# An earlier first search, one-hots in one comparison per quarter, and a new place for the first expert in the plan

## The chip, the cores and the metric

The kernel runs on one core of a Trainium2 chip. The metric is the device time of one execution in microseconds: 1155.01 us is the median of three runs (1153.06, 1155.01 and 1155.10). TensorE (PE) multiplies, VectorE (DVE), ScalarE (ACT) and GpSimd (POOL) do elementwise work, and SyncE (SP) issues most of the transfers. Each engine takes its instructions in the order in which they were written to its queue.

## The reference

Three layers follow one another. Attention with a sink and a window gives `x` for N = 3072 tokens of 512 features. A dense layer `x = g(x @ w_in) @ w_out` follows. The last one shares the tokens out to 8 experts of 384 tokens each, which this change is about:

```python
    cap = N // E
    logits = x @ w_gate
    order = np.argsort(-flat)                  # flat = logits.flatten()
    for idx in order:
        tok, e = (int(idx) // E, int(idx) % E)
        if assigned[tok] >= 0 or counts[e] >= cap:
            continue
        assigned[tok] = e
        counts[e] += 1
    ...
        h = np.maximum(x[mask] @ w1[e], 0.0)
        out[mask] = h @ w2[e]
```

## The kernel before

The tokens go through the dense layer in 12 blocks of 256 (`moe1_steps`). A block makes 16 hidden pieces `f` (`hid`: 12 products into `hp`, then VectorE, ScalarE and GpSimd make `u` and its parts `gh` and `gl`) and adds each piece's share of the outcome (`proj`: 12 products into `up`, in a low and a high half of the columns; the high half also holds the logits). Every fp32 product is done as three products of rounded parts. The last block first makes only its logits (`gate`, `logits`), and its outcome (`rows`) is made while the first search runs. The rows go to a table in memory, `x2d` (`done`).

The tokens of one expert are found by a search (`phase`). `values` (`v`) and `owners` (`own`) take each token's best logit and its expert. Seven rounds narrow a threshold down: `compare` (`ind`, 768 comparisons in a partition), `count` (`pg`, six products), `counts` (`cnt`), `total` (`pc`), `bound` (`hit` to `th`). Then `above`, `loads`, `choose` and `rank` choose the expert whose share is full and number its tokens, `places`, `slots` (`oh`, a one-hot matrix of 128 places for each of 24 tiles) and `look` (`pk`, 24 products) turn the numbers into a list, `tokens` (`tok`) writes it as integers, and `retire` takes these tokens and the expert out of the logits for the next search. `gather` has GpSimd fetch the 384 rows (`xg`), `turn` turns them round on TensorE (`xt`) and splits them (`xsh`, `xsl`). `weight` loads an expert's weights (`w1r`, `w2r`) and splits them into a high and a low part: the low part (`w1l`, `w2l`) either by VectorE (`rest`) or by a transfer that adds to a negated copy (`minus`, `add`). `expert` multiplies (`hp`, then `us`) and `store` writes the rows out.

Eight experts run after one another, and the search of the next stands between the products of the one before. `experts` sets that order with a table of times: `at(t, step)` puts a step at time t of a plan, the plan is sorted, and in what `at` enters every engine keeps the sorted order. The times only set an order; how long something takes is not in them. `T[k]` is the place of expert k's first product, `PERIODS` the length of an expert, `SECOND` the place of the second search after the first one's end, `CHAIN` the distance from one search to the next. The products of the last two blocks and the first search are entered without that rule: there the building layer sorts by its own priorities. `unread` writes products that nobody reads (`idle`) where TensorE has no work.

Of the kernel before, what the change touches and what calls it, by code (L numbers as in the profile page):

```python
# [7 lines left out]
F32 = mybir.dt.float32  # L8
# [48 lines left out]
FIND = 21.5  # L57
PERIODS = [39.5] * (E - 2) + [37.0, 33.5]

SECOND, CHAIN, EARLY = 11.3, 34.8, 59.0  # L60
# [7 lines left out]
NQ = 4  # L68

# [5 lines left out]
class Kernel:  # L75
# [547 lines left out]
    def moe1_steps(self, blk, xs, hold=None, part=None):  # L623
# [5 lines left out]
        fa, fz = part or (0, FT)  # L629
        hps, ahead = {}, blk > 1  # L630
# [17 lines left out]
        def hid(f):  # L648
# [22 lines left out]
        def proj(f):  # L671
            gh, gl = st.pop(f)
            assert f in self.have_out
            if f == fa:
# [68 lines left out]

        store = [(0.0, lambda: done(0)), (0.0, lambda: done(1))]
        second = gate if hold else proj
# [10 lines left out]
        rest = []  # L756
# [10 lines left out]
    def pools2(self, e):  # L767
        tc = self.tc
        self.oh = e(tc.tile_pool(name="oh", bufs=1))
        self.ex = e(tc.tile_pool(name="ex", bufs=2))  # L770
        self.ew = e(tc.tile_pool(name="ew", bufs=2))

    def router_consts(self):
# [8 lines left out]
        self.nrow = rt.tile([P, P], BF16, name="nrow")  # L782
# [15 lines left out]
        self.t_row = rt.tile([P, GT], F32, name="t_row")  # L798
        nc.vector.tensor_copy(self.t_row, fl[:, 0, :GT])
# [20 lines left out]
    def phase(self, last, out, first=False):  # L820
# [5 lines left out]
        def values():  # L826
            v = st["v"] = self.rw.tile([P, GT], F32, name="v")
            nc.vector.tensor_reduce(out=v, in_=lm, axis=AX.X, op=OP.max)
# [4 lines left out]
        def owners():  # L833
            st["own"] = self.rw.tile([P, GT, E], BF16, name="own")
            nc.vector.tensor_tensor(out=st["own"], in0=lm, in1=st["v"].unsqueeze(2).to_broadcast([P, GT, E]),
                                    op=OP.is_equal)
# [4 lines left out]
        def compare(r):  # L841
            n = 1 << ROUNDS[r][1]
            th = st["th"] if r else self.pat[0]
            ge = st["ind"] = self.rw.tile([P, GT, n], BF16, name="ind", tag=f"ind{n}")
            nc.vector.tensor_tensor(out=ge, in0=st["v"].unsqueeze(2).to_broadcast([P, GT, n]),  # L845
                                    in1=th.bitcast(F32).unsqueeze(1).to_broadcast([P, GT, n]), op=OP.is_ge)
# [8 lines left out]
        def count(r):  # L855

            n = 1 << ROUNDS[r][1]
            pg = st["pg"] = self.psum([g * n, g * E], self.rtag, "pg")
            for t in range(0, GT, g):
# [108 lines left out]
        def places():  # L968
# [6 lines left out]
            nc.vector.scalar_tensor_tensor(a, a, -float(P), z, op0=OP.mult, op1=OP.add)  # L975
# [5 lines left out]
            st["oh"] = self.oh.tile([P, GT, P], BF16, name="oh", bufs=1)  # L981
            st["a"] = a
            st["pk"] = self.psum([P, 6], "A", "pk")
# [3 lines left out]
        def slots(h):  # L987
            for t in range(n_ * h, n_ * h + n_):
                nc.vector.tensor_scalar(st["oh"][:, t], self.nrow, st["a"][:, t:t + 1], None, op0=OP.is_equal)  # L989

        def look(h):
            for t in range(n_ * h, n_ * h + n_):
                nc.tensor.matmul(st["pk"], st["oh"][:, t], st["rr"][:, t].rearrange("p x c -> p (x c)"),
                                 start=(t == 0), stop=(t == GT - 1))
                if first and t < GT - 1:
                    self.unread(1, 5 * 32)
            if h == NQ - 1:
                st["tf"] = self.rw.tile([P, 3], F32, name="tf")
                nc.scalar.copy(st["tf"], st["pk"][:, 0:3])
# [8 lines left out]
    def weight(self, cur, i, first):  # L1008
# [4 lines left out]
        dma = name == "w2" or (first and c == 0)  # L1013
# [64 lines left out]
    def expert(self, cur):  # L1078
# [6 lines left out]
        def up(f):  # L1085
# [5 lines left out]
            def part(i):  # L1091
                w_, x_ = ((wl, xh), (wh, xl), (wh, xh))[i]
# [59 lines left out]
    def experts(self, plan, start):  # L1152
# [17 lines left out]
        def find(k, ph, t):  # L1170
# [8 lines left out]
            for r in range(len(ROUNDS)):  # L1179
# [4 lines left out]
                at(t + 1.0, ph["count"], r)  # L1184
                free.append(t + 1.05)
                at(t + 1.35 + GAP, ph["counts"], r)
                free.append(t + 1.45 + GAP)
                at(t + 1.6 + GAP, ph["total"], r)
                at(t + 2.05 + 2 * GAP, ph["bound"], r)
# [4 lines left out]
        for k in range(E):  # L1194
            cur, ph = curs[k], self.phase(k + 1 == E, curs[k], k == 0)
            if k == 0:

                steps = [(1.0, ph["values"]), (1.0, ph["owners"])]
                for r in range(len(ROUNDS)):
                    steps += [(1.0, lambda r=r, f=ph[n]: f(r)) for n in ("compare", "count", "counts", "total", "bound")]  # L1200
# [353 lines left out]
```

## Time and profile before

| | |
|---|---|
| median of three runs | 1155.01 us |
| profiled execution | 1155.79 us |
| its span in the profile | 1154.0 us |
| TensorE busy | 1103.5 us, 96% |
| VectorE busy | 871.4 us, 76% |
| ScalarE busy, GpSimd busy | 698.9 us, 486.5 us |

Times in the rows are microseconds from the start of the span. The first 760 us are attention and the dense layer. The last block's hidden pieces run to about 787, the first search from 791 to 825, the first expert from 833, the second from 877, and the last product ends shortly after 1147. A bracket at the end of a row tells how long the engine was idle before it, and what it was released by. Some products overlap in these rows, so that the distance of two starts tells more than a duration.

### The profile page before, as it was taken

How to read it: one execution, taken by the hardware profiler on the slowest of the kernel's cores; microseconds unless marked ns; L12 is line 12 of the kernel's file. 1: busy time of each engine (PE TensorE's matmuls, PEld its weight loads, DVE VectorE, ACT ScalarE, POOL GpSimd, SP SyncE). 2: the span in 40 equal slices, each digit the busy share in tenths (PEclk: the TensorE clock that was granted, in tenths of full speed). 3: DMA queues.
4: the chain of work that ended last, by engine and by line, in shares of the span. 5: the costliest groups of instructions: out<-in, count | busy, mean ns of one | idle time of the engine just before them, and what ended most of it. 6: DMA issues, size and time to landing. Idle time of an engine off the chain costs nothing.

```text
span 1154.0 us, 24267 instructions
## 1 busy us (share of the span) xinstructions
PE 1103.5 (96%) x8212; PEld 1008.3 (87%) x8212; DVE 871.4 (76%) x2718; ACT 698.9 (61%) x1596; POOL 486.5 (42%) x590
## 2 busy tenths in 40 slices
PE   5899988999999999999999999999899999999997
PEld 3678878999999999999999999997578788888896
DVE  5878888787887878787878787755788888889430
ACT  4788777666776766676767776642245435444552
POOL 1335655545554545555545555541222322332321
PEclk9899999999999999999999999999999999999999
DMA  4655622222322222323222322000576768677872
GB/s 106 158 149 164 160 65 53 57 57 45 69 49 59 36 57 47 71 47 65 35 55 49 71 47 54 13 20 10 147 209 182 214 181 207 178 207 196 228 209 67
DMA packets 241928, 118.13 MB, mean 102 GB/s; under 512 B 196096, under 2 KB 220672, under 8 KB 241792
## 3 DMA queue, kind: packets, MB, share of 16 engines
q1 hardware_dynamic: 231504, 85.36, 29.2%
q0 software_dynamic: 8592, 29.89, 11.0%
q8 instruction: 67, 1.10, 0.4%
q10 hardware_dynamic: 1696, 1.22, 0.4%
q14 instruction: 69, 0.57, 0.2%
HBM read 86.00 MB, written 13.11 MB: 86 GB/s over the span
## 4 chain that ended last, share of the span: by engine, by line
PE 55%; DVE 13%; issue 7%; DMA 4%; ACT 4%; POOL 3%; SPq 1%; POOLq 0%; DVEq 0%; ACTq 0%
PE hp L644 16%; PE up L682 14%; PE us L1121 6%; PE hp L1094 6%; PE xp L391 3%; PE up L691 2%; PE tp L372 2%; DVE ks L301 2%; PE sc L334 1%; PE sc L335 1%; DVE oh L989 1%; SPq L426 1%; DVE ind L845 1%; DVE u L665 1%; DMA qr<-in_q_dram 1%
## 5 line engine op out<-in xcount | busy, mean ns | idle before, releaser
L669 POOL TENSOR_TENSOR gl<-u,gh 128x256 fp32r<-128x256 f32 x192 | 152.8, 796 | 183.4 <-ACT gh L668 159.5
L682 PE MATMUL up<-woh,gl 128*128 128x256 f32 (+1 forms) x528 | 152.7, 289 | 2.6 <-POOL gl L669 2.6
L682 PE MATMUL up<-woh,gh 128*128 128x256 f32 (+1 forms) x528 | 150.0, 284 | 0.0
L682 PE MATMUL up<-wol,gh 128*128 128x256 f32 (+1 forms) x528 | 149.7, 284 | 0.0
L666 ACT ACTIVATE u<-u,half 128x256 f32<-128x256 f32 x192 | 97.4, 508 | 75.7 <-DVE u L665 71.4
L644 PE MATMUL hp<-xh,wil 128*128 128x256 f32 x768 | 131.6, 289 | 1.0 <-POOL wil L246 0.6
L644 PE MATMUL hp<-xl,wih 128*128 128x256 f32 x768 | 127.6, 283 | 1.1 <-POOL xl L412 0.9
L644 PE MATMUL hp<-xh,wih 128*128 128x256 f32 x768 | 127.3, 283 | 0.0
L644 PEld LDWEIGHTS hp<-xh,wil 128*128 128x128 f32 x768 | 107.2, 190 | 2.3 <-POOL wil L246 0.8
L644 PEld LDWEIGHTS hp<-xl,wih 128*128 128x128 f32 x768 | 106.8, 190 | 2.0 <-POOL xl L412 2.0
L644 PEld LDWEIGHTS hp<-xh,wih 128*128 128x128 f32 x768 | 107.6, 191 | 0.0
L667 DVE TENSOR_TENSOR u<-hp,u 128x256 f32<-128x256 f32 x192 | 80.4, 419 | 31.1 <-ACT u L666 28.8
L682 PEld LDWEIGHTS up<-woh,gl 128*128 128x128 f32 x528 | 99.9, 189 | 3.1 <-POOL gl L669 3.1
L665 DVE TENSOR_SCALAR u<-hp 128x256 f32<-128x256 f32 x192 | 80.1, 418 | 27.3 <-PE hp L644 20.1
L682 PEld LDWEIGHTS up<-wol,gh 128*128 128x128 f32 x528 | 99.5, 188 | 0.4 <-issue 0.4
L682 PEld LDWEIGHTS up<-woh,gh 128*128 128x128 f32 x528 | 99.5, 188 | 0.4 <-issue 0.4
L668 ACT CAST gh<-u 128x256 fp32r<-128x256 f32 x192 | 77.5, 404 | 29.5 <-DVE u L667 26.6
L353 POOL TENSOR_TENSOR pr<-pr,sm 128x576 f32<-128x576 f32 x56 | 65.5, 1170 | 68.3 <-DVE ks L307 29.7
L339 ACT ACTIVATE pr<-pr,sm 128x288 f32<-128x288 f32 (+1 forms) x160 | 85.3, 534 | 12.7 <-DVE sm L337 11.6
L1102 ACT ACTIVATE hh<-hp 128x384 fp32r<-128x384 f32 x64 | 31.5, 492 | 101.0 <-PE hp L1094 87.9
L1121 PE MATMUL us<-w2h,hl 128*128 128x512 f32 x192 | 80.7, 420 | 0.0
L1121 PE MATMUL us<-w2h,hh 128*128 128x512 f32 x192 | 75.6, 394 | 0.0
(278 smaller groups left out, 3056.7 us busy)
## 6 DMA issues: line engine op xcount, KB each, us to landing
w1r<-in_moe_w_dram SPq DMA_DIRECT2D x32, 512.0 KB, 4.7
w2r<-in_moe_w_dram SPq DMA_DIRECT2D x32, 512.0 KB, 4.4
w2l<-w2r POOLq DMA_DIRECT2D x32, 512.0 KB
qr<-in_q_dram SPq DMA_DIRECT2D x320, 32.0 KB, 2.0
dr<-in_moe_w_in_dram SPq DMA_DIRECT2D x15, 512.0 KB, 4.1
dr<-in_moe_w_out_dram SPq DMA_DIRECT2D x15, 512.0 KB, 3.7
x2d<-ev SPq DMA_DIRECT2D x26, 256.0 KB, 2.2
vr<-in_v_dram SPq DMA_DIRECT2D x56, 96.0 KB, 2.4
```

The source lines that it names most:

```text
L339: nc.scalar.activation(pr, pr, AF.Exp, bias=sm[:, 0, u:u + 1], scale=-1.0, accum_out=sm[:, 1, u:u + 1])
L353: nc.gpsimd.tensor_tensor(out=pr, in0=pr, in1=r.unsqueeze(2).to_broadcast([P, 2, 2 * P + NS]), op=OP.mult)
L391: nc.tensor.matmul(o_, l, r, start=(i == 0), stop=(i == len(mm) - 1), skip_group_check=True)
L644: nc.tensor.matmul(ps, w_[:, k, fs], x_[:, k, :], start=not done, stop=len(done) == 11, skip_group_check=ahead)
L665: nc.vector.tensor_scalar(u, ps, -1.0, 1.0, op0=OP.max, op1=OP.min)
L666: nc.scalar.activation(u, u, AF.Square, bias=self.half, scale=0.5)
L667: nc.vector.tensor_tensor(out=u, in0=ps, in1=u, op=OP.max)
L668: nc.scalar.copy(gh, u)
L669: nc.gpsimd.tensor_tensor(out=gl, in0=u, in1=gh.bitcast(F32), op=OP.subtract)
L682: nc.tensor.matmul(o, g_[:, ts], self.w_out_part(w_, f)[:, cs], start=(f == fa and i == 0 and (cs.start > 0 or t == 0)), stop=(f == fz - 1 ...
L1094: nc.tensor.matmul(ps, w_[:, k, fs], x_[:, k, :], start=(i == 0 and k == 0), stop=(i == 2 and k == 3))
L1121: nc.tensor.matmul(us[j], h_[:, o], w_[:, f % 2, :], start=(f == 0 and i == 0), stop=(f == nf - 1 and i == 2))
```

## The change

Seven edits go together.

1. In the last but one block, the low halves of `proj` for the last three pieces are left for later (`late`), and its logits are stored with the high half (`half`). The last block's first three `gh` and `gl` move to a free pair of `x` buffers.
2. The first search takes `values`, `owners`, the first `compare` and five of the six first `count` products of 22 tiles ahead of the last block's logits, and the other two tiles when they are there.
3. For the first expert the one-hots are made by four comparisons of 128 x 6 elements against a table `slot` (four copies on ScalarE) instead of 24 of 128 elements, in fp16; a one-hot's columns are then 24 elements apart. For every expert `rr` holds the token number as one fp16 number, so that `look` has 3 columns instead of 6, and a copy through ScalarE (`tf`) and one GpSimd instruction go.
4. For the first expert, `retire` stands behind `tokens` and `gather`.
5. The first expert's first `w1l` is made by VectorE instead of by a transfer through GpSimd's queue, and in its first four pieces the products with both high parts come first.
6. The first expert's products start at 39.4 in the plan instead of 42.8 and are spread up to the same place of the second expert (82.3).
7. The second search stands 0.8 later, the third where it was. The first round's count and what follows it in that round stand 0.6 later in the third and later searches.

```diff
-FIND = 21.5
+FIND, KNOWN = 21.5, 15.0
-SECOND, CHAIN, EARLY = 11.3, 34.8, 59.0
+SECOND, CHAIN, EARLY = 12.1, 34.8, 59.0
+XT, LEAD, NEXT, BACK = 35.0, 39.4, 82.3, 0.8
+LATE = 3
...
@@ moe1_steps
+        split = blk == NB - 2
...
-            if hold and f >= 3:
-                gh, gl = (hold().tile([P, TB], F32R, name="g" + x, tag="g" + x, bufs=FT - 3) for x in "hl")
+            if hold and f < LATE:
+                if f == 0:
+                    st["spare"] = [self.xp.tile([P, 4, TB], F32R, name="gs" + x, tag="x" + x) for x in "hl"]
+                gh, gl = (t[:, f] for t in st["spare"])
...
                 for o, cs in ((us[2][:, t], slice(0, hw)), (us[t], slice(hw, DX))):
+                    if (cs.start == 0) if split and f >= FT - LATE and not low else (cs.start > 0 and low):
+                        continue
...
-            nc.scalar.copy(lg, st["lg"])
+            self.copied = nc.scalar.copy(lg, st["lg"]).ins
...
+        def half(t, x):
+            ev = self.mo.tile([P, DM], F32, name="ev", tag="ev")
+            cs = slice(x * hw, (x + 1) * hw)
+            if x:
+                (nc.vector.tensor_copy if t else nc.scalar.copy)(ev[:, cs], us[t][:, :hw])
+                nc.vector.tensor_copy(self.logits[:, 2 * blk + t, :], us[t][:, hw:])
+            else:
+                nc.scalar.copy(ev[:, cs], us[2][:, t])
+            r = blk * TB + t * P
+            nc.sync.dma_start(self.x2d[r:r + P, cs], ev[:, cs])
...
+        if split:
+            store = [(0.0, lambda t=t: half(t, 1)) for t in range(2)]
+            self.late = [lambda f=f: proj(f, True) for f in range(FT - LATE, FT)]
+            self.late += [(0.0, lambda t=t: half(t, 0)) for t in range(2)]
...
-        rest = []
+        rest = list(self.late)
@@ pools2
+        self.slot = self.oh.tile([P, P, GT], F16, name="slot", bufs=1)
+        with tc.issue_after(self.copied):
+            for i in range(0, P, 32):
+                self.nc.scalar.copy(self.slot[:, i:i + 32],
+                                    self.nrow[:, i:i + 32].unsqueeze(2).to_broadcast([P, 32, GT]))
@@ phase: values, owners, compare, count take a range of tiles (a, b)
...
-            rr = st["rr"] = self.rw.tile([P, GT, 2, 3], BF16, name="rr")
-            nc.gpsimd.tensor_scalar(rr[:, :, 0].rearrange("p t c -> p c t"), bs, self.pcol, None, op0=OP.mult)
-            nc.gpsimd.tensor_tensor(out=rr[:, :, 1].rearrange("p t c -> p c t"), in0=bs,
-                                    in1=self.t_row.unsqueeze(1).to_broadcast([P, 3, GT]), op=OP.mult)
+            rr = st["rr"] = self.rw.tile([P, GT, 3], F16, name="rr")
+            nc.gpsimd.tensor_tensor(out=rr.rearrange("p t c -> p c t"), in0=bs,
+                                    in1=self.tok.unsqueeze(1).to_broadcast([P, 3, GT]), op=OP.mult)
...
         def slots(h):
+            ts = slice(n_ * h, n_ * h + n_)
+            if first:
+                nc.vector.tensor_tensor(out=st["oh"][:, :, ts], in0=self.slot[:, :, ts],
+                                        in1=st["a"][:, ts].unsqueeze(1).to_broadcast([P, P, n_]), op=OP.is_equal)
+                return
...
-                nc.tensor.matmul(st["pk"], st["oh"][:, t], st["rr"][:, t].rearrange("p x c -> p (x c)"),
+                nc.tensor.matmul(st["pk"], st["oh"][:, :, t] if first else st["oh"][:, t], st["rr"][:, t],
                                  start=(t == 0), stop=(t == GT - 1))
-                if first and t < GT - 1:
-                    self.unread(1, 5 * 32)
...
+            if first and h < NQ - 1:
+                self.unread(1, 5 * 32)
...
-            nc.vector.scalar_tensor_tensor(out["tok"], st["pk"][:, 3:6], float(P), st["tf"], op0=OP.mult, op1=OP.add)
+            nc.vector.tensor_scalar(out["tok"], st["pk"], float(N // 2), None, op0=OP.add)
@@ weight, expert
-        dma = name == "w2" or (first and c == 0)
+        dma = name == "w2"
...
-                w_, x_ = ((wl, xh), (wh, xl), (wh, xh))[i]
+                w_, x_ = ((wl, xh), (wh, xl), (wh, xh))[2 - i if lead and f < 4 else i]
@@ experts
+                s = t + (0.6 if r == 0 and k > 1 else 0.0)
-                at(t + 1.0, ph["count"], r)
+                at(s + 1.0, ph["count"], r)
...
+                known = 2 * (NB - 1)
+                for i, nm in enumerate(("values", "owners", "compare", "count")):
+                    x = (0,) * (i > 1) + (0, known if i < 3 else known // 4 * 4)
+                    plan.at(start - KNOWN + i, lambda f=ph[nm], x=x: f(*x))
...
-                for dt, n in ((4.3, 10), (11.6, 8), (15.4, 4), (16.9, 2), (18.2, 2), (20.1, 3)):
+                for dt, n in ((4.3, 10), (9.9, 12), (15.1, 3), (16.6, 3)):
...
+                    at(t + 0.15, ph["tokens"])
+                    at(t + 0.2, self.gather, cur)
+                    at(t + 0.25, ph["retire"])
+                    g, step = start + XT, 1.5
+                    T.append(start + LEAD)
...
+                            at(start + FIND + SECOND - 0.2 + 0.01 * u, rest, u)
+            if k == 0:
+                d = (start + NEXT - T[0]) / len(steps)
+                T[0] = start + NEXT - PERIODS[0]
+            first = T[k] if k else start + LEAD
...
-                t = max(t, began + CHAIN)
+                t = max(t, began + CHAIN) - (BACK if k == 1 else 0.0)
```

On VectorE, behind the first expert's one-hots (`oh`), before:

```order
L975 SCALAR_TENSOR_TENSOR a<-a,z 128x24
L989 TENSOR_SCALAR oh<-nrow,a 128x128 x24
L962 TENSOR_SCALAR pe<-est 128x8
L963 TENSOR_TENSOR pt<-ge 128x24
L964 TENSOR_SCALAR pt<-pt 128x24
L965 TENSOR_TENSOR logits<-logits,pe 128x192
L966 TENSOR_TENSOR logits<-logits,pt 128x192
L1003 SCALAR_TENSOR_TENSOR tok<-pk,tf 128x3
L828 TENSOR_REDUCE v<-logits 128x24
```

The same place now (`pe`, `pt` and `logits` are `retire`):

```order
L1012 SCALAR_TENSOR_TENSOR ah<-a,z 128x24
L1024 TENSOR_TENSOR oh<-slot,ah 128x128x6 x4
L1039 TENSOR_SCALAR tok<-pk 128x3
L998 TENSOR_SCALAR pe<-est 128x8
L999 TENSOR_TENSOR pt<-ge 128x24
L1000 TENSOR_SCALAR pt<-pt 128x24
L1001 TENSOR_TENSOR logits<-logits,pe 128x192
L1002 TENSOR_TENSOR logits<-logits,pt 128x192
L1081 TENSOR_TENSOR w1l<-w1r,w1h 128x512 x2
L860 TENSOR_REDUCE v<-logits 128x24
```

`tok` moved ahead of `retire`, and two `w1l` now stand between `retire` and the second search's `v`.

On TensorE, from the first expert's last turned rows (`xt`) to its first products (`hp`) and the count of the second search beside them (`pg`), before:

```order
L1070 MATMUL xt<-ident,xg 128x128 x4
L818 LDWEIGHTS one
L818 MATMUL idle<-one 128x512
L818 LDWEIGHTS one
L818 MATMUL idle<-one 128x512
L818 LDWEIGHTS one
L818 MATMUL idle<-one 128x512
L860 LDWEIGHTS ind
L860 MATMUL pg<-own,ind 128x32
```

The same place now; this count is the second round's, while the one before was the third's:

```order
L1106 MATMUL xt<-ident,xg 128x128 x4
L849 LDWEIGHTS one
L849 MATMUL idle<-one 128x512
L849 LDWEIGHTS one
L849 MATMUL idle<-one 128x512
L849 LDWEIGHTS one
L849 MATMUL idle<-one 128x512
L1130 MATMUL hp<-xsh,w1h 128x384 x4
L896 LDWEIGHTS ind
L896 MATMUL pg<-own,ind 128x32
```

A first group of products moved ahead of the count, and the search stands one round earlier against the expert.

On TensorE at the end of the first expert, ahead of the third search's first count (`us` are the second products of the expert), before:

```order
L1121 MATMUL us<-w2h,hl 128x512
L1121 MATMUL us<-w2l,hh 128x512
L1121 MATMUL us<-w2h,hh 128x512
L1094 MATMUL hp<-xsh,w1l 128x384 x4
L860 LDWEIGHTS ind
L860 MATMUL pg<-own,ind 128x32
```

The same place now, behind the last look-up product (`pk`) of the second search:

```order
L1032 MATMUL pk<-rr,oh 128x3
L1130 MATMUL hp<-xsh,w1l 128x384 x4
L1130 MATMUL hp<-xsl,w1h 128x384 x4
L1130 MATMUL hp<-xsh,w1h 128x384 x4
L896 LDWEIGHTS ind
L896 MATMUL pg<-own,ind 128x32
```

Two groups of the last hidden piece moved ahead of that count.

## Rows read from the trace of the kernel before

**Rows 1.** Busy time by stage, all engines; columns: us, then busy per engine, PEclk, DMA
```profile
837.00:877.00 40.00, 38.47 (x263) 30.89 (x263) 34.19 (x135) 19.00 (x27) 9.97 (x11) 1.00 0.74 205
...
877.00:917.00 40.00, 39.33 (x276) 31.86 (x275) 33.62 (x138) 16.86 (x26) 9.74 (x12) 1.00 0.70 190
```

**Rows 2.** TensorE in order of time; columns: start, us, what, count, idle before and releaser
```profile
763.90 0.74 PE L644 MATMUL hp<-xh,wil 128*128 128x256 f32 x4
...
817.11 0.16 PE L941 MATMUL po<-tot,tri 128*128 128x2 bf16 x1 [2.29 <-DVE tot L936]
...
817.16 3.83 PE L818 MATMUL idle<-one 128*128 128x512 bf16 x10
...
833.31 0.32 PE L860 MATMUL pg<-own,ind 128*128 128x32 bf16 x6 [0.27 <-DVE ind L845]
833.48 0.94 PE L1094 MATMUL hp<-xsh,w1l 128*128 128x384 f32 x4
...
842.48 0.85 PE L1094 MATMUL hp<-xsl,w1h 128*128 128x384 f32 x4
843.17 0.86 PE L1094 MATMUL hp<-xsh,w1h 128*128 128x384 f32 x4
...
863.85 0.32 PE L860 MATMUL pg<-own,ind 128*128 128x32 bf16 x6 [0.74 <-DVE own L835]
...
876.57 0.95 PE L1094 MATMUL hp<-xsh,w1l 128*128 128x384 f32 x4
```

**Rows 3.** VectorE in order of time, from the last block to the third search
```profile
763.42 0.42 DVE L667 TENSOR_TENSOR u<-hp,u 128x256 f32<-128x256 f32 x1 [0.63 <-ACT u L666]
...
791.72 0.35 DVE L828 TENSOR_REDUCE v<-logits 128x24 f32<-128x192 f32 x1
...
792.38 0.95 DVE L845 TENSOR_TENSOR ind<-v,pat 128x768 bf16<-128x768 f32 x1
...
794.62 0.17 DVE L881 TENSOR_SCALAR_CACHE_REDUCE hit<-pc 128x8 bf16<-128x8 f32 x1 [0.47 <-PE pc L873]
...
819.21 4.17 DVE L989 TENSOR_SCALAR oh<-nrow,a 128x128 bf16<-128x128 bf16 x24
823.30 0.20 DVE L962 TENSOR_SCALAR pe<-est 128x8 f32<-128x8 bf16 x1
...
824.05 0.36 DVE L966 TENSOR_TENSOR logits<-logits,pt 128x192 f32<-128x192 f32 x1
824.55 0.16 DVE L1003 SCALAR_TENSOR_TENSOR tok<-pk,tf 128x3 int32<-128x3 f32 x1
824.62 0.34 DVE L828 TENSOR_REDUCE v<-logits 128x24 f32<-128x192 f32 x1
...
836.64 0.69 DVE L1045 TENSOR_TENSOR w1l<-w1r,w1h 128x512 fp32r<-128x512 f32 x1
...
862.18 0.34 DVE L828 TENSOR_REDUCE v<-logits 128x24 f32<-128x192 f32 x1
```

**Rows 4.** Groups by tile; durations are min/median/max ns, then first and last start
```profile
L372 PEld LDWEIGHTS tp<-ident,pr x296: 194/209/219, 164.0 to 746.2; 128*128 128x128 f32 x148
...
L214 PEld LDWEIGHTS gp<-ident,df x64: 138/140/230, 39.6 to 174.5; 128*128 128x128 f32 x64
...
L993 PEld LDWEIGHTS <-oh x48: 95/96/151, 820.4 to 860.7; 128*128 128x128 bf16 x48
...
L926 DVE TENSOR_TENSOR w<-own,est x2: 257/258/259, 815.5 to 852.0; 128x192 bf16<-128x192 bf16 x2
```

**Rows 5.** TensorE alone, 1 us stretches after 816
```profile
818.00:819.00 1.00, 1.00 (x4) 0.50 0.60 106
```

**Rows 6.** GpSimd in order of time, the first gather
```profile
825.00 1.07 POOL L1056 DMA_INDIRECT xg<-x2d,tok  x1 [1.49 <-DVE v L828]
```

**Rows 7.** VectorE alone, from the second search's start to the third's
```profile
824.60:862.20 37.60, 31.88 (x131) 1.00 0.86 228
```

**Rows 8.** TensorE's waits from 833 to 877: us in total, times, longest
```profile
PE pg L860 <- DVE ind L845: 0.9, 3, 0.3
```

More of the change, by code (lines that the diff above doesn't have):

```diff
@@ L669, in hid, with proj @@
             nc.gpsimd.tensor_tensor(out=gl, in0=u, in1=gh.bitcast(F32), op=OP.subtract)
-        def proj(f):
-            gh, gl = st.pop(f)
+        def proj(f, low=False):
             assert f in self.have_out
+            gh, gl = st[f] if split and f >= FT - LATE else st.pop(f)
             if f == fa:
@@ L797, in router_consts @@
         nc.vector.tensor_scalar(self.e_rev, fl[:, 0, :E], -1.0, float(E), op0=OP.mult, op1=OP.add)
-        self.t_row = rt.tile([P, GT], F32, name="t_row")
-        nc.vector.tensor_copy(self.t_row, fl[:, 0, :GT])
+        self.tok = rt.tile([P, GT], F32, name="tok_row")
+        nc.vector.tensor_scalar(self.tok, fl[:, 0, :GT], float(P), self.pcol, op0=OP.mult, op1=OP.add)
+        nc.vector.tensor_scalar(self.tok, self.tok, float(-N // 2), None, op0=OP.add)
         self.pat = []
@@ L824, in phase, with values @@
         R = len(ROUNDS)
-        def values():
-            v = st["v"] = self.rw.tile([P, GT], F32, name="v")
-            nc.vector.tensor_reduce(out=v, in_=lm, axis=AX.X, op=OP.max)
+        def values(a=0, b=GT):
+            if a == 0:
+                st["v"] = self.rw.tile([P, GT], F32, name="v")
+            nc.vector.tensor_reduce(out=st["v"][:, a:b], in_=lm[:, a:b], axis=AX.X, op=OP.max)
             if last:
@@ L831, in values, with owners, compare @@
                 nc.vector.memset(st["tau"], DEAD / 2)
[L833 to L836, printed above, removed]
+        def owners(a=0, b=GT):
+            if a == 0:
+                st["own"] = self.rw.tile([P, GT, E], BF16, name="own")
+            nc.vector.tensor_tensor(out=st["own"][:, a:b], in0=lm[:, a:b],
+                                    in1=st["v"][:, a:b].unsqueeze(2).to_broadcast([P, b - a, E]), op=OP.is_equal)
         g = 4
-        def compare(r):
+        def compare(r, a=0, b=GT):
             n = 1 << ROUNDS[r][1]
             th = st["th"] if r else self.pat[0]
-            ge = st["ind"] = self.rw.tile([P, GT, n], BF16, name="ind", tag=f"ind{n}")
-            nc.vector.tensor_tensor(out=ge, in0=st["v"].unsqueeze(2).to_broadcast([P, GT, n]),
-                                    in1=th.bitcast(F32).unsqueeze(1).to_broadcast([P, GT, n]), op=OP.is_ge)
+            if a == 0:
+                st["ind"] = self.rw.tile([P, GT, n], BF16, name="ind", tag=f"ind{n}")
+            nc.vector.tensor_tensor(out=st["ind"][:, a:b], in0=st["v"][:, a:b].unsqueeze(2).to_broadcast([P, b - a, n]),
+                                    in1=th.bitcast(F32).unsqueeze(1).to_broadcast([P, b - a, n]), op=OP.is_ge)
             if r + 1 == R:
@@ L853, in compare, with count @@
                                         op=OP.bitwise_xor)
-        def count(r):
+        def count(r, a=0, b=GT):
             n = 1 << ROUNDS[r][1]
-            pg = st["pg"] = self.psum([g * n, g * E], self.rtag, "pg")
-            for t in range(0, GT, g):
+            if a == 0:
+                st["pg"] = self.psum([g * n, g * E], self.rtag, "pg")
+            pg = st["pg"]
+            for t in range(a, b, g):
                 nc.tensor.matmul(pg, st["ind"][:, t:t + g].rearrange("p t n -> p (t n)"),
@@ L1076, in turn, with expert @@
         return turned, rest
-    def expert(self, cur):
+    def expert(self, cur, lead):
         nc, a, tc = self.nc, self.a, self.tc
@@ L1183, in find @@
                     t -= 0.7
-                at(t + 1.0, ph["count"], r)
[L1185 to L1189, printed above, removed]
+                s = t + (0.6 if r == 0 and k > 1 else 0.0)
+                at(s + 1.0, ph["count"], r)
+                free.append(s + 1.05)
+                at(s + 1.35 + GAP, ph["counts"], r)
+                free.append(s + 1.45 + GAP)
+                at(s + 1.6 + GAP, ph["total"], r)
+                at(s + 2.05 + 2 * GAP, ph["bound"], r)
                 t += 2.95 + 2 * GAP + (0.6 if r == 0 else 0.0)
@@ L1225, in experts @@
                     at(t, ph["slots"], h)
-                    at(t + 0.7, ph["look"], h)
-                    t += 0.6
-                at(t, ph["retire"])
-                at(t + 1.2, ph["tokens"])
-                at(t + 1.3, self.gather, cur)
-                t += 1.3
-                g, step = t + 5.2, 1.3
-                T.append(max(T[-1] + PERIODS[k - 1], g + 4.9) if k else g + 4.9)
+                    at(t + (0.7 if k else 0.5), ph["look"], h)
+                    t += 0.6 if k else 0.4
+                if k:
+                    at(t, ph["retire"])
+                    at(t + 1.2, ph["tokens"])
+                    at(t + 1.3, self.gather, cur)
+                    t += 1.3
+                    g, step = t + 5.2, 1.3
+                    T.append(max(T[-1] + PERIODS[k - 1], g + 4.9))
+                else:
+                    at(t + 0.15, ph["tokens"])
[3 more added lines that the diff above has]
+                    T.append(start + LEAD)
                 if T[k] - 6.2 > g:
@@ L1257, in experts @@
                 at(g + step * j, turned)
-                filler(g + step * j + 1.2, 0.8, lambda tr=tr: tr["f"][1]())
+                if k:
+                    filler(g + step * j + 1.2, 0.8, lambda tr=tr: tr["f"][1]())
+                else:
+                    at(g + step * j + 1.2, lambda tr=tr: tr["f"][1]())
             x = p + W0
```

48 lines of the change are left out of this document (27 added, 21 removed).

## The prediction

> **What bounds the kernel now.** I read the page first (its 40 slices), then TensorE's busy time by stage, then TensorE and VectorE in order of time around the change. By stage, from 837 to 877, while the first expert runs, TensorE is busy 38.47 us of 40, from 877 to 917 39.33 [rows 1], so that only its idle time and its fillers can be saved. The hole lies ahead of that: between the last block's products and the first expert's first product at 833.48 [rows 2] stand the first search, the look-up of its tokens, the gather and filler products. While the first expert runs, the second search runs on VectorE, from its `v` at 824.62 to the third search's `v` at 862.18, 37.56 us [rows 3]; TensorE takes that search's counts in written order, and at the third search's first count it has waited 0.74 us for VectorE's `own` [rows 2]. So two lines run side by side: TensorE's products, and the searches. What the end gains is what the later of the two gains. That is the question of this change.
>
> **Part 1, the last two blocks.** The low halves of three hidden pieces move back 18 products of 256 columns. In the built order 15 of them stand right ahead of the last block's third hidden piece, and only three come after its last one. That third piece started at 763.90, when VectorE's maximum of 763.42 + 0.42 had freed its bank [rows 2, 3]. In the new order both maxima stand behind an eviction of the block before, so I put this piece 0.3 us later; the five early counts cost TensorE 0.2, two evictions on ScalarE ahead of the last rounding 0.1. Bounds for the logits: 0.4 earlier (three products and no wait) to 0.9 later. I take +0.6. That the logits come sooner is thus not what the order shows. The 0.9 us early comparison fits into VectorE's gaps there.
>
> **Part 2, the first round.** From `v` (791.72) to `hit` (794.62) it took 2.90 us; the comparison alone ran 0.95 on 768 elements [rows 3]. With 2 of 24 tiles left, `v`, `own` and `ind` take some 0.65 us instead of 1.61, and one product instead of six is counted: 1.5 in all, -1.4. Six rounds stay as they are. Net after part 1: -0.8. The one-hots start at 819.21 - 0.8 = 818.4.
>
> **Part 3, one-hots and look-up.** Now 24 one-hots take 4.17 us [rows 3]. Four comparisons of 768 fp16 elements replace them. The fp32 comparison gives one end: 0.95 each, 3.6 us in a pipelined row. `w` on 192 bf16 elements, also broadcast in the middle, takes 0.258 [rows 4]; taking the fixed 0.16 that 0.95 leaves over 0.79 for 768, its 192 went at twice the rate. I take the near row: 0.55 each, 0.48 apart, done at 820.4. ScalarE's new table (four copies) waits for an early product of the last block's second row tile, so it is done long before; if it came last it would cost its 3 to 4 us in full.
> TensorE then becomes the limit. Its 10 fillers took 3.83 us, at half clock: 0.50 was granted from 818 to 819, after it had stood idle for 2.29 us [rows 2, 5]. The last block's products now end later (+0.7) and `po` stands sooner (-0.8), so the idle time shrinks to about 0.8 and I expect full clock: fillers from 816.3 to 818.7. Then 24 products at 0.097 (a weight load of 95 ns, [rows 4]) and three short fillers: from 819.0 to 821.6, `tok` at 821.75 instead of 824.55, -2.8. The copy through ScalarE and `retire` (823.30 to 824.41, [rows 3]) no longer stand ahead of it.
> The unknown here is the weight load of a one-hot whose columns are now 48 bytes apart. The nearest strided row is the fp32 transposes of `pr` (every second word): 209 ns against 140 for the packed ones of `df` [rows 4], a factor 1.5. Bounds: 0.097 and 0.145 per product, 1.2 us later; more under the rivals. I take 0.097, the row of the same type and size. The Trainium skill, "TensorE: Matmul & The Clock Gate", section "Weight-path perf modes", says that the fast load is on for 128 weights that are not FP32 and reads its columns packed or strided; by that the stride is free and the sum stays, by the fp32 rows it is 1.2 us worse. No 16-bit strided load is in this trace.
>
> **Part 4, gather and first product.** The gathers go out 0.3 after `tok`, as before (825.00, [rows 6]): 822.2. From there to the first product were 8.48 us, of which some 0.4 was the wait for a count that stood ahead of it [rows 2]; the high parts now come first. First product at 822.2 + 8.1 = 830.3, -3.1.
>
> **Part 5, the second search.** Behind `tok` VectorE now has `retire`, 1.1, and the two halves of `w1l`, 0.69 each [rows 3], 1.2 pipelined, that a DMA had done; then `v`, at 821.75 + 2.5 = 824.3: -0.3 only. From there to the third `v` VectorE has the same list of work as before (seven rounds, the choice and the one-hots, 3 `xsl`, 6 `w1l`, 7 `hl`), in another interleaving: more of the expert's pieces in the first four rounds, fewer in the last three. I take 37.6 us plus 0.5 for rounds in which it now waits behind a product; bounds -2 (less idle time) and +1. Third `v`: +0.2.
>
> **Part 6, what reaches the end.** TensorE comes 3.1 us sooner and meets the search's counts in written order. Each of the second search's counts from the second round on now stands one round earlier against the expert's products, so TensorE waits for `ind` 0.3 to 0.8 us in five or six of them. At the third search's first count two groups of products more now stand ahead of it (0.69 each, from 842.48 to 843.17, [rows 2]); from that count to the second expert's first product were 876.57 - 863.85 = 12.72 us, now 11.3 if it never waits. But the second expert starts behind that search's fourth count, and VectorE runs those rounds 0.2 late less one `hl` (0.5). So the second expert starts between 1.2 and 0 sooner; I take -0.45. After it the stretches are full [rows 1], so this shift is kept.
> The later first-round counts: 0.74 us was waited at the first of these [rows 2], already used above; the others can give back 0 to 1.0 together. I take -0.5.
>
> **The sum** against the profiled execution (1155.79, span 1154.0): -0.45 - 0.5 = -0.95. The median shown, 1155.01, is 0.78 below that execution; I put the sum on the median: 1154.1. What can be told from no change here is about 0.2%, 2.3 us.
>
> **Rivals.**
> *A, the lead reaches the end (faster).* VectorE was busy 31.88 us of the 37.6 between the two `v` [rows 7]; if the interleaving uses 2 to 3 of the idle 5.7, TensorE is not held. Then the second expert starts 3.1 sooner, less 0.5 for the count and total of the round that now lies behind the first product, and with -0.5 from later counts the time is 1155.0 - 3.1 = 1151.9. For it: both lines wait on each other now. Against it: 0.74 at the third search's count.
> *B, strided loads (slower).* `tok` and with it the second search are late by 24 (c - 0.097), c being the time of one look-up product. The second expert's shift is about 24 (c - 0.097) - 0.45, so the whole is slower by 2.3 from c = 0.23 on; at 0.3 it is 1154.1 + 4.9 = 1159. For it: the fp32 factor. Against: 16-bit loads are half as long.
> *C, the first search is no sooner.* The half clock stays, or the comparisons run at the fp32 rate (0.4 more apart): `tok` is 1.1 instead of 2.8 sooner, the second search 1.4 later than before, and all after it 1.7 later than forecast: 1155.8, within no change.
>
> **Chances.** Forecast and C together 0.53, A 0.31 (whatever makes the search gain 2 us counts with it), B and other losses 0.16. So faster by over 0.2% 0.31, within 0.53, slower 0.16. The range runs from 1151.4 (A with all of the later counts) to 1157.2 (B at c = 0.225); the forecast's own is 1152.8 to 1156.2.
>
> **What would show it.** Right: `tok` 2 to 3 us sooner after the last logits, first product about 3 sooner, third `v` within 1 us of 862.2, TensorE's waits for `ind` in the first expert up from 0.9 us [rows 8] to 3 or 4. Wrong: the third `v` 2 us sooner (A), or look-up products 0.2 us apart (B). A half clock after 816 would show part 3 wrong.

## The result and the profile after

| | before | changed |
|---|---|---|
| median of 6 runs each, us | 1153.66 | 1160.93 (1159.36 to 1162.02) |
| ratio | | 1.0057, interval 1.0046 to 1.0068 |
| span of the profiled execution, us | 1154.0 | 1160.2 |

The changed kernel is slower, 6.6 us by the ratio; 1154.1 was forecast, with 1157.2 as the upper end. The forecast was put on a median before of 1155.01 us, which six runs put at 1153.66, so the miss is better read from the ratio.

TensorE by stage in the changed kernel (columns as in [rows 1]):

```profile
837.00:877.00 40.00, 34.83 (x241) 27.22 (x240) 31.71 (x126) 14.74 (x21) 7.94 (x9) 1.00 0.60 167
...
877.00:917.00 40.00, 38.50 (x267) 31.27 (x267) 34.54 (x139) 16.69 (x24) 9.27 (x10) 1.00 0.71 192
```

While the first expert runs TensorE now does 34.83 us of work in 40 instead of 38.47 [rows 1]: 3.6 us more of idle time. TensorE in order of time, changed kernel (columns as in [rows 2]):

```profile
791.16 0.29 PE L722 MATMUL lt<-ident,lgs 16*128 16x16 f32 x2
...
815.98 0.16 PE L977 MATMUL po<-tot,tri 128*128 128x2 bf16 x1 [0.79 <-DVE tot L972]
816.03 2.32 PE L849 MATMUL idle<-one 128*128 128x512 bf16 x10
819.00 0.56 PE L1032 MATMUL pk<-rr,oh 128*128 128x3 f16 x6 [0.65 <-DVE oh L1024]
...
820.95 4.43 PE L849 MATMUL idle<-one 128*128 128x512 bf16 x12
825.96 0.63 PE L1106 MATMUL xt<-ident,xg 128*128 128x128 f32 x4 [0.58 <-issue]
826.42 0.30 PE L896 MATMUL pg<-own,ind 128*128 128x32 bf16 x6
...
830.48 0.97 PE L1130 MATMUL hp<-xsh,w1h 128*128 128x384 f32 x4
...
840.62 0.24 PE L909 MATMUL pc<-cnt,pile 128*128 128x8 f16 x4 [1.28 <-DVE cnt L902]
...
855.05 0.17 PE L948 MATMUL pe<-ce,one 128*128 128x8 bf16 x1 [1.72 <-DVE ce L944]
...
879.56 0.95 PE L1130 MATMUL hp<-xsh,w1l 128*128 128x384 f32 x4
```

The list is sooner, as planned: the first look-up product starts at 819.00, the first expert's first product at 830.48 instead of 833.48 [rows 2]. Then TensorE waits 1.28 us at 840.62 and 1.72 at 855.05; before, its longest wait while the first expert ran was 0.74 us, at the third search's first count [rows 2]. And the second expert starts at 879.56 instead of 876.57 [rows 2]. VectorE in order of time, changed kernel:

```profile
793.53 0.17 DVE L917 TENSOR_SCALAR_CACHE_REDUCE hit<-pc 128x8 bf16<-128x8 f32 x1 [0.47 <-PE pc L909]
...
818.30 2.15 DVE L1024 TENSOR_TENSOR oh<-slot,ah 128x768 f16<-128x768 f16 x4
821.13 0.16 DVE L1039 TENSOR_SCALAR tok<-pk 128x3 int32<-128x3 f32 x1 [0.68 <-PE pk L1032]
...
823.51 0.34 DVE L860 TENSOR_REDUCE v<-logits 128x24 f32<-128x192 f32 x1
...
839.32 0.56 DVE L1143 SCALAR_TENSOR_TENSOR hl<-hp,hh 128x384 fp32r<-128x384 f32 x1 [1.03 <-ACT hh L1138]
...
840.39 0.18 DVE L902 CAST cnt<-pg 128x32 f16<-128x32 f32 x1
...
852.75 0.56 DVE L1143 SCALAR_TENSOR_TENSOR hl<-hp,hh 128x384 fp32r<-128x384 f32 x1 [2.58 <-ACT hh L1138]
...
865.74 0.35 DVE L860 TENSOR_REDUCE v<-logits 128x24 f32<-128x192 f32 x1
```

The second search, from `v` at 823.51 to the third's at 865.74, takes 42.23 us, not 37.56 [rows 3]. VectorE alone in this stretch (columns as in [rows 7]):

```profile
823.50:865.75 42.25, 31.94 (x130) 0.99 0.71 194
```

It has as much work as before, 31.94 us against 31.88 [rows 7]; all that the search is longer by is waiting. VectorE waits in it for ScalarE's `hh`, 1.03 us at 839.32 and 2.58 at 852.75, and did not before; its `cnt` of 840.39, for which TensorE's `pc` waits, stands behind the first of these `hl` (and a `w1l`). ScalarE in order of time, changed kernel:

```profile
837.84 1.06 ACT L1067 ACTIVATE w2l<-w2r 128x1024 fp32r<-128x1024 f32 x1 [2.27 <-DMA w2r<-in_moe_w_dram]
838.81 0.47 ACT L1138 ACTIVATE hh<-hp 128x384 fp32r<-128x384 f32 x1
...
850.33 1.06 ACT L1067 ACTIVATE w2l<-w2r 128x1024 fp32r<-128x1024 f32 x1 [5.80 <-DMA w2r<-in_moe_w_dram]
851.29 1.04 ACT L1073 CAST w2h<-w2r 128x1024 fp32r<-128x1024 f32 x1
852.23 0.48 ACT L1138 ACTIVATE hh<-hp 128x384 fp32r<-128x384 f32 x1
```

Each of these `hh` stands behind a `w2l` that waits for a transfer of `w2r`, 2.27 and 5.80 us. The second of these transfers, in SyncE's order of time, and SyncE's waits for GpSimd's adding transfers from 826 to 856 (us in total, times, longest):

```profile
843.74 0.37 SPq L1058 DMA_DIRECT2D w2r<-in_moe_w_dram  x1
```

```profile
SPq L1058 <- DMA w2l<-w2r: 6.6, 1, 6.6
```

It went out at 843.74, after 6.6 us in which SyncE waited for its buffer: GpSimd's adding transfer, most likely that of the second `w2` piece (issued at 839.20), had to land first. In the kernel before, and in e2 below, SyncE waits in the same stretch for VectorE's `w1l` instead, and at most 0.4 us for an adding transfer:

```profile
SPq L1022 <- DVE w1l L1045: 5.9, 2, 3.0
```

```profile
SPq L1058 <- DVE w1l L1081: 6.4, 2, 3.3
```

So the early place changed which reader the last load's buffer has to wait for. That the four raw buffers are handed out in the order in which their last readers stand is inferred from this.

Which kernel loses where is read best from the last block's logits on (start of their transposes `lt`, 791.16 here and 790.97 in the first profile of before): up to there the executions differ by themselves, 788.8 to 792.0 us, whatever the kernel. From `lt` on, in us (T1 is the second expert's first product, "last" the start of the last product; the ratio is to the kernel before, with its interval):

| kernel | `lt` to `tok` | second `v` to third | `lt` to T1 | T1 to last | ratio |
|---|---|---|---|---|---|
| before | 33.6 | 37.55 | 85.6 | 270.5 | |
| before, second profile | 33.4 | 37.45 | 85.3 | 270.6 | |
| changed | 30.0 | 42.24 | 88.4 | 273.9 | 1.0057 (1.0046 to 1.0068) |
| changed, second profile | 30.0 | 41.51 | 87.7 | 273.9 | |
| e1_own_buffer | 30.0 | 39.95 | 86.9 | 273.8 | 1.0051 (1.0038 to 1.0065) |
| e2_hh_ahead | 30.0 | 39.19 | 85.3 | 273.8 | 1.0046 (1.0030 to 1.0062) |
| e3_no_shift | 29.9 | 41.56 | 87.7 | 271.7 | 1.0050 (1.0032 to 1.0067) |
| e4_shift_alone | 33.4 | 38.54 | 86.4 | 273.1 | 1.0029 (1.0018 to 1.0039) |
| e5_hh_ahead_no_shift | 29.9 | 39.84 | 86.0 | 271.6 | 1.0012 (1.0002 to 1.0021) |
| e6_old_place | 30.0 | 40.85 | 87.6 | 271.2 | 1.0024 (1.0010 to 1.0037) |
| e7_search_later | 29.9 | 40.88 | 86.2 | 273.9 | 1.0038 (1.0024 to 1.0051) |
| e8_w1l_behind | 29.9 | 41.56 | 86.5 | 271.6 | 1.0014 (1.0006 to 1.0023) |
| e9_count_ahead | 29.9 | 38.93 | 85.0 | 271.5 | 1.0013 (1.0000 to 1.0026) |
| e10_search_first | 30.0 | 40.32 | 85.9 | 271.1 | 1.0020 (1.0011 to 1.0029) |

So the changed kernel is 3.4 to 3.6 us sooner at `tok`, 2.1 to 3.1 later at T1, and loses 3.3 to 3.4 more behind it: two losses at two places.

### The profile page after: what moved, and what is told of

It reads as the page before. It is cut to its first block, busy times and chain, and to the rows that moved or that the text cites. A ratio compares the mean times of both kernels' runs of the same rounds, so it can differ in the third digit from the quotient of the medians.

```text
span 1160.2 us, 24190 instructions
## 1 busy us (share of the span) xinstructions
PE 1104.0 (95%) x8191; PEld 1007.2 (87%) x8191; DVE 872.7 (75%) x2703; ACT 701.9 (60%) x1592; POOL 482.7 (42%) x581
## 4 chain that ended last, share of the span: by engine, by line
PE 53%; DVE 14%; issue 7%; ACT 4%; DMA 4%; POOL 3%; SPq 1%; POOLq 0%; DVEq 0%; ACTq 0%
PE hp L648 16%; PE up L692 14%; PE hp L1130 6%; PE us L1157 5%; PE xp L394 3%; PE up L701 2%; PE tp L375 2%; DMA w2r<-in_moe_w_dram 2%; PE sc L337 2%; PE sc L338 1%; DVE ks L304 1%; DVE w1l L1081 1%; DVE oh L1028 1%; DVE ind L879 1%; DMA w2l<-w2r 1%
## 5 line engine op out<-in xcount | busy, mean ns | idle before, releaser
L1077 POOL DMA_DIRECT2D w2l<-w2r x32 | 29.5, 923 | 112.8 <-ACT w2l L1067 110.7
```

## The experiments

**e1 and e2: the late weights.**

```diff
e1:
-            st["r"] = self.ew.tile(shape, F32, name=name + "r", tag="er", bufs=4)
+            own = first and (c, name) == (3, "w2")
+            st["r"] = self.ew.tile(..., tag="er0" if own else "er", bufs=1 if own else 4)
e2:
-                    a1 = T[0] + (0.0, 2.9, 0.0, 3.6, 5.6, 7.8, 10.0, 13.0)[i]
+                    a1 = T[0] + (0.0, 2.9, 0.0, 3.6, 7.4, 7.8, 10.0, 16.5)[i]
```

Expected of e1: 

> The changed kernel, with a raw buffer of its own for the first expert's last w2 piece, so that its load no longer waits until another piece's accumulating transfer has landed. Theory W (weights: ScalarE stands at the late w2 pieces, the expert's hh behind it, VectorE's hl behind that, and the second search behind hl): the last w2r goes out by 838 instead of 843.7, ScalarE's wait of 5.80 us shrinks below 2, VectorE's 2.58 us wait for hh near 850 goes, the third search's v comes 2.4 us sooner (863.3 instead of 865.74), the second expert's first product at 877.2 instead of 879.56, the time 1158.5. Theory F (the second search is long because more of the expert's pieces stand in its first rounds on VectorE): third v within 0.5 of 865.7, time within 1 us of 1160.9.

Expected of e2: 

> The changed kernel, with the first expert's second and fourth w2 pieces 1.8 and 3.5 later in the plan, so that on ScalarE the second and the fifth hh stand ahead of the work that waits for those weights. Theory W: both waits of VectorE for hh (1.03 and 2.58 us) go, the third v comes 3.5 to 4 us sooner (about 862), the second expert's first product at 875.9, the time 1157.2 (the later experts' loss stays). Theory F: third v within 0.5 of 865.7 and the time within 1 us of 1160.9.

SyncE and VectorE in order of time, e1:

```profile
834.73 0.94 SPq L1059 DMA_DIRECT2D w2r<-in_moe_w_dram  x2
```

```profile
837.17 0.56 DVE L1144 SCALAR_TENSOR_TENSOR hl<-hp,hh 128x384 fp32r<-128x384 f32 x1 [0.69 <-ACT hh L1139]
...
847.92 0.53 DVE L1144 SCALAR_TENSOR_TENSOR hl<-hp,hh 128x384 fp32r<-128x384 f32 x1
```

Both last `w2r` go out by 835.7, the wait at the fifth `hh` is gone, and 0.69 us of the other is left. VectorE, e2:

```profile
837.64 0.55 DVE L1143 SCALAR_TENSOR_TENSOR hl<-hp,hh 128x384 fp32r<-128x384 f32 x1
...
848.40 0.53 DVE L1143 SCALAR_TENSOR_TENSOR hl<-hp,hh 128x384 fp32r<-128x384 f32 x1
...
862.17 0.35 DVE L860 TENSOR_REDUCE v<-logits 128x24 f32<-128x192 f32 x1
```

With `hh` ahead of the late weights both waits are gone. Against the two profiles of the changed kernel the search takes 1.6 to 2.3 us less in e1 and 2.3 to 3.0 less in e2, and T1 comes 0.7 to 1.5 and 2.4 to 3.1 sooner. So theory W (late weights) holds in the traces, and F (more of the expert's pieces in the search's first rounds) falls as the main cause, though 1.6 us of the longer search stay in e2. The medians, 1159.1 and 1158.6, fell by less than expected (1158.5 and 1157.2); with intervals of 1.5 and 1.9 us to either side they are not clear of the changed kernel, and it takes e5 to show the gain in the time.

**e3 and e4: the shifted count.**

```diff
e3 (e4 is the reverse, in the kernel before):
-                s = t + (0.6 if r == 0 and k > 1 else 0.0)
+                s = t
                 at(s + 1.0, ph["count"], r)
                 free.append(s + 1.05)
...
```

Expected of e3: 

> The changed kernel with the first round's count of the third and later searches back at its old place (the 0.6 undone). Theory S (this shift costs the later experts some 0.7 to 1.0 us each): the second expert's first product stays at 879.6, the distances of the later experts' first products go from 42.5, 41.0, 41.6, 41.0 back to some 41.8, 40.3, 40.6, 40.0, the time 1157.6. Theory P (the later loss is the second search's lateness passed on): the time within 0.8 us of 1160.9.

Expected of e4: 

> The kernel before with the 0.6 shift of the first round's count of the third and later searches alone. Theory S: 2.5 to 3.5 us slower than before, 1156.2 to 1157.2. Theory P: within 0.8 us of before, 1153.7. By my forecast's step: 0.5 faster.

The shift alone, put into the kernel before, costs 2.6 us behind T1 and 1.0029 in all (1157.0); taking it out of the changed kernel gives 2.2 back behind T1 (1158.5). So S holds (the shift itself costs the later experts), and my step (0.5 faster) is wrong in sign. One place where it sits, VectorE and TensorE around the sixth search's first count, while the fourth expert runs and the fifth's tokens are looked up, changed kernel:

```profile
986.15 0.19 DVE L902 CAST cnt<-pg 128x32 f16<-128x32 f32 x1 [2.37 <-PE pg L896]
986.26 1.06 DVE L1028 TENSOR_SCALAR oh<-nrow,a 128x128 f16<-128x128 f16 x6
987.23 0.16 DVE L917 TENSOR_SCALAR_CACHE_REDUCE hit<-pc 128x8 bf16<-128x8 f32 x1
```

```profile
986.87 0.68 PE L1032 MATMUL pk<-rr,oh 128*128 128x3 f16 x6
...
991.21 0.24 PE L909 MATMUL pc<-cnt,pile 128*128 128x8 f16 x4 [0.37 <-DVE cnt L902]
```

and without the shift:

```profile
980.18 2.04 DVE L1028 TENSOR_SCALAR oh<-nrow,a 128x128 f16<-128x128 f16 x12
983.37 0.19 DVE L902 CAST cnt<-pg 128x32 f16<-128x32 f32 x1 [1.15 <-PE pg L896]
...
984.41 0.17 DVE L917 TENSOR_SCALAR_CACHE_REDUCE hit<-pc 128x8 bf16<-128x8 f32 x1 [0.39 <-PE pc L909]
```

```profile
985.02 0.31 PE L1032 MATMUL pk<-rr,oh 128*128 128x3 f16 x6
...
988.41 0.24 PE L909 MATMUL pc<-cnt,pile 128*128 128x8 f16 x4
```

Without the shift VectorE makes twelve one-hots while it has nothing to do between `own` and the first `cnt`. With it, the free places that the plan hands to such pieces move too (`free` is counted from `s`): six of these one-hots stand ahead of the search's `v` and six behind `cnt`, and VectorE is idle 2.37 us ahead of `cnt` instead of 1.15. Counted from the fourth expert's first product, `v` comes 18.46 us behind instead of 17.48. TensorE then takes the look-up at the pace of the one-hots (0.68 us instead of 0.31) and waits for the next `cnt` (0.37), and from one expert's first product to the next the fourth and the fifth expert take 41.64 and 41.03 us, against 40.56 and 39.99 before. This is read from the traces; the later count and the moved one-hots were not tried apart.

**e5: both together.** Expected: 

> The edits of e2_hh_ahead and e3_no_shift together. If W (late w2 on ScalarE, 2.3 us) and S (the shift, 2.4 us) are separate losses: they add, 1156.2, with 53.0 us from the second search's v to the second expert's first product and 203.9 from there to the sixth expert's. Rival: one hides the other (the later experts are late only because the second search is, or the reverse): 1157.5 or more. Either way some 2.5 us over before stay open.

In the traces they add: up to T1 e5 gains as e2 does, and behind it as e3 does; 357.5 us from `lt` to the last product against 362.3 and 361.6. The ratio, 1.0012, is clear of that of the changed kernel and of e2 and e3, each of which lacks one of the two edits. (The ratios of e2 and e3 alone would give a sum of 1.0039, but they are uncertain by 0.0016 to 0.0018 each.) What is left over before is 1.4 us: 0.4 to 0.7 up to T1, 0.7 in the second expert (T1 to the third's first product 42.50, before 41.77) and 0.4 in the fifth. The part up to T1 may be no loss at all: e2, with the same edits there, has T1 at 85.3 as before, and e5's profile is one with a long way from `tok` to the first product (see e11 and e12). In the second expert one `w1l` half (0.68 us) now stands ahead of the fourth search's second `ind`, and TensorE waits 0.43 us for that, and 0.32 at the third search's `po`; this is read from the two traces and was not tried. The fp16 one-hots and the narrower look-up of the later experts show no loss: the third, fourth and sixth expert take 40.28, 40.65 and 40.02 us in e5, before 40.27, 40.56 and 40.18.

**e6 and e7: other places in the plan.**

```diff
e6 (on e3):
-XT, LEAD, NEXT, BACK = 35.0, 39.4, 82.3, 0.8
+XT, LEAD, NEXT, BACK = 35.0, 42.8, 82.3, 0.8
e7 (on e5):
-SECOND, CHAIN, EARLY = 12.1, 34.8, 59.0
+SECOND, CHAIN, EARLY = 13.1, 34.8, 59.0
```

Expected of e6: 

> The changed kernel without the shift, and with the first expert's first product back at 42.8 in the plan (its products and weights at their old places; the sooner search, one-hots, tokens and gather stay). Theory R (what loses is the early place: weights late on ScalarE, TensorE at the search's counts before VectorE): no late w2 in front of an hh, 38.0 us from the second v to the third, the second expert's first product about 1 us sooner than before, the later loss 1.1, together 1153.5, as before. Rival Q (the loss lies in what was moved ahead of the second search, or in the fp16 one-hots of the later experts): 1156 or more.

Expected of e7: 

> e5_hh_ahead_no_shift with the second search and the later ones 1.0 later in the plan. If TensorE loses there because it meets the search's counts before VectorE has ind ready (about 2.9 us of waits in the first expert): these waits fall below 1.5, the first expert's 45.9 us from its first product to the next expert's first go to about 44.5, time 1.5 under e5. Rival: the search then ends later and its tokens hold the second expert: the time as e5 or up to 1 us more.

Neither came out as hoped. In e6 the second search takes 40.85 us, not 38.0, and the time, 1156.4, is in the range of rival Q, so the early place is not all of the loss. What else it is e6 doesn't tell: the half clock that lies on fillers in the changed kernel falls on products of the first expert here (a group of four takes 1.63 us at 832.09 instead of 0.94). In e7 TensorE's waits in the first expert only moved (1.5 us at `pc` instead of 1.0 at the third search's first `pg`), and 2.3 us were lost behind T1, in the second and the third expert (43.91 and 41.46 us, in e5 42.50 and 40.28).

**e8, e9, e10: what the second search stands behind.**

```diff
e8 (on e5):
-                            at(start + FIND + SECOND - 0.2 + 0.01 * u, rest, u)
+                            at(start + FIND + SECOND + 1.4 + 0.01 * u, rest, u)
e9 (on e5):
-XT, LEAD, NEXT, BACK = 35.0, 39.4, 82.3, 0.8
+XT, LEAD, NEXT, BACK = 36.3, 39.4, 82.3, 0.8
-                    g, step = start + XT, 1.5
+                    g, step = start + XT, 1.15
e10 (on e5): SECOND 11.3, XT 35.5, BACK 0.0, the first w1l at SECOND + 4.9, the first xsl 1.2 later
```

Expected of e8: 

> e5_hh_ahead_no_shift with the first w1l (1.34 us on VectorE) behind the second search's own instead of ahead of its v. If VectorE's list ahead of the second search is what holds it: v 1.3 us sooner and the third v and the time 1.2 us sooner than e5. Rival: the first count stands behind the first xt on TensorE, which waits for the gather, and VectorE stood idle 1.66 us for that count: v sooner by 1.3, third v and time within 0.5 us of e5.

Expected of e9: 

> e5_hh_ahead_no_shift with the first expert's xt 1.3 later in the plan, so that on TensorE the second search's first count and total stand ahead of the first xt, which waits for the gather, as in the kernel before. Theory X (that place costs the second search 2.3 us: in e5 its first count starts 2.90 behind v and its second ind 6.34 behind, before 1.69 and 4.06): first count at v + 1.7, second ind by v + 5, from the second v to the third 38.0 us instead of 39.84, the second expert's first product 1.5 sooner, time 1.5 under e5. Rival: the search is sooner, but TensorE waits for it no less, or xt and the first product come later by as much: within 0.5 of e5.

Expected of e10: 

> As e9_count_ahead by another way, and further: e5_hh_ahead_no_shift with the second search at its old place in the plan (11.3), ahead of the first xt on TensorE, the first w1l on VectorE behind that search's second ind instead of ahead of its v, and the first xsl behind it too. Theory X: v 1.2 sooner as well, 37.6 us from the second v to the third, the second expert's first product 2.5 sooner than e5's, time 2.5 under e5 and so 1 under the kernel before. Rival: the later searches, whose places stay, hold the second expert's tokens: as e9.

In the changed kernel TensorE has `xt`, then `pg` (825.96, 826.42 above): the second search's first count waits for the gather. In e8 `v` is 1.2 sooner and the search 1.7 longer, and the time is that of e5 (1.0014), so nothing is won: the rival of e8 holds. e9, TensorE from the fillers on:

```profile
822.81 0.30 PE L896 MATMUL pg<-own,ind 128*128 128x32 bf16 x6
...
823.83 0.63 PE L1106 MATMUL xt<-ident,xg 128*128 128x128 f32 x4 [0.19 <-issue]
...
827.80 0.98 PE L1130 MATMUL hp<-xsh,w1h 128*128 128x384 f32 x4 [0.68 <-ACT xsh L1107]
828.62 0.32 PE L896 MATMUL pg<-own,ind 128*128 128x32 bf16 x6
```

The first count now stands 1.72 us behind `v` (821.09) instead of 2.90, and the search is 0.9 shorter and T1 0.95 sooner than in e5: half of the 1.5 to 1.8 expected, and nothing of it shows in the time (1.0013, e5 1.0012). Even this half is not shown to come from the edit. The way from `tok` to the first product took 9.08 us in e9's profile and 10.09 in e5's; against e2, whose second search stands in e5's order and where it took 9.42, the search is 0.3 shorter and T1 0.3 sooner, no more than two profiles of one kernel differ. The second count has taken over, behind the first `hp` (828.62), which waits for the same gather. e10 shows it once more: `v` 1.2 sooner, and T1 where e5 has it. No version came out faster than the kernel before; the best, e5 and e9, are 1.0012 and 1.0013.

**e11 and e12: how far a profile repeats.** 

> The kernel before, profiled a second time, to see how far one profile's stretches repeat. If the stretch behind the last logits repeats to within 0.3 us, it is 356.0 again (from the last logits' transpose to the last product) with 85.5 to the second expert's first product; if the gather's landing moves it, up to 1 us more or less.

 

> The changed kernel, profiled a second time. If the stretch behind the last logits repeats: 362.2 to the last product, 88.3 to the second expert's first product, VectorE's wait of 2.6 us for the fifth hh again; else the differences of about 3 us that single profiles showed are not to be trusted.

The stretch behind T1 repeats to 0.1 us and the one up to `tok` to 0.2; T1 moves by 0.3 and 0.7. In the changed kernel it moves with the way from `tok` to the first expert's first product, which holds the gather: 9.35 us in the first profile and 10.12 in the second. This way is either short or long, also in kernels whose edits lie behind it: 9.24 in e1 and 9.42 in e2, 10.15 in e3 and 10.09 in e5; in the kernel before 8.93 and 9.03, in e4 10.00. What decides it is open. So 1 us at T1 read from two profiles is doubtful; 2 us and more is not, nor is what lies behind T1. Like with like, `hh` ahead of the late weights brings T1 3.1 us sooner when the way is short (88.4 to 85.3 in e2) and 1.7 when it is long (87.7 to 86.0 in e5).

## Why the prediction was wrong

- **Parts 1 to 3 came out, with one miss.** `lt` to `hit` 2.4 us instead of 3.65 (-1.3, forecast -1.4); four one-hots in 2.15 (forecast 2.0); `tok` 3.4 to 3.6 sooner against the logits (forecast 3.4). The half clock did not go, which the prediction had named as a sign against part 3. It lies behind `tok` now, on the fillers, where nothing waits for it. The 0.6 for the logits can't be told from the spread of `lt`.
- **Part 4 met its number in part by luck.** The first product came at 830.48 (forecast 830.3). But the gather went out 1.13 us behind `tok` (822.26, the row below), not 0.45 as before, and from `tok` to the first product it took 9.35 and 10.12 us, not the 8.55 of the sum; the number was met because `tok` stood at 821.13 and not at 821.75. The gather's row names `retire`'s `logits` as its releaser, although `retire` was moved behind the gather; the cause was not tried.
- **Part 5 failed.** "From there to the third `v` VectorE has the same list of work ... I take 37.6 us plus 0.5", bounds -2 and +1: it took 42.2 and 41.5. The list of work was the same (31.94 us busy, before 31.88); the term that failed is the 0.5 us for waiting, which measured 4.6 and 3.9. I counted VectorE's own work and asked where TensorE waits for VectorE. Not priced was what stands ahead of the search's products and of `hl` on the other engines. `w2l` ahead of `hh` on ScalarE is 2.3 to 3.0 us of the longer search by e2 against the two profiles, 1.7 by e5 against e3. Of the 1.6 left in e2, `xt` ahead of the first `pg` is 0.3 by e9 against e2, and at most 0.9 (against e5); the rest is open. Both orders can be read from the built program.
- **Part 6 failed with it.** T1 came 2.1 to 3.1 later, not 0.45 sooner. TensorE's long waits were at `pc` and `pe`, for the search; at `ind` they rose from 0.9 us only to 1.8 (second row below; forecast 3 to 4).
- **The later counts, -0.5,** were +2.2 to +2.6 (e3, e4). I priced the wait that the shift takes away, not the one-hots that move with it.

```profile
822.26 1.17 POOL L1092 DMA_INDIRECT xg<-x2d,tok  x1 [4.10 <-DVE logits L1001]
```

```profile
PE pg L896 <- DVE ind L879: 1.8, 4, 0.8
```

- **The rivals.** None was it. B had the sign, but the look-up products came 0.07 us apart, far from its 0.23. A is refuted: the lead of 3 us never passed the second search. C is refuted too, as `tok` was sooner by all that was forecast. What happened fell to the "other losses", which had 0.16 together with B and no mechanism.

## What to carry to other kernels

When an expert, a tile or a stage is started sooner, ask of every engine that it uses which of its instructions waits for a transfer, and what stands behind that one: a weight that comes no sooner than before blocks everything written behind it on that engine (5.80 us on ScalarE here). In a plan with shared free places, a step that is moved by half a microsecond deals these places anew; compare the whole order of the engine, not the step. A lead is worth only as much as the later of the two lines that meet at the next stage.

## What the runs showed of the hardware

One-hots as weights, by tile, changed kernel: the first expert's, with columns 48 bytes apart, and all later ones, packed (durations min/median/max ns):

```profile
L1032 PEld LDWEIGHTS <-oh x24: 148/176/188, 819.0 to 820.8; 128*128 128x128 f16 x24
...
L1032 PEld LDWEIGHTS <-oh x144: 95/96/102, 860.9 to 1069.0; 128*128 128x128 f16 x144
```

A strided 16-bit load of 128 columns takes 176 ns, a packed one 95, at the same full clock, and look-up products with all one-hots at hand start 70 ns apart instead of 25. The Trainium skill, "TensorE: Matmul & The Clock Gate", section "Weight-path perf modes", has the fast load on for 128 weights that are not FP32, "packed or strided". In this trace the strided load is nearly twice as long at this stride, and the measurement decides. It cost 24 x 0.045 = 1.1 us of TensorE here, hidden behind the making of the one-hots (2.15 us) but for the last six products.

The clock again: TensorE alone, one stretch of 1 us in the changed kernel:

```profile
822.00:823.00 1.00, 1.00 (x3) 0.50 0.00 0
```

A share of 0.50, the lower of its two levels (1.2 of 2.4 GHz), was granted from 821 to 824, after TensorE had stood idle 0.79 and 0.65 us since 815; in the kernel before it lay ahead of the look-up, after 2.29 us [rows 2, 5]. Which work it falls on moved with the order, and in e6 it fell on products that counted.
